# A recurrent transformer block with streamed weights: the residual in a home of its own, a larger GpSimd descriptor scratch, a quarter of an output unit kept in SBUF, and other places for the streamed units

## The chip, the cores and the metric

The kernel runs on one core of a Trainium2 chip. Its time is the device time of one execution in microseconds. Three executions before the change took 1982.02 us (median; 1969.82 to 1986.7).

## What is computed

`x` has 2048 rows of 1024 numbers, in bfloat16. It is layer-normalised to `xn`. Two branches are added to it. Branch B is a dense layer, a GELU and a second dense layer. Branch A goes through the rows in 64 segments of 32, one after the other: eight memory rows that the segment before left are put ahead of its rows, 32 heads of 128 attend over the 40 rows, and the first eight rows of the result are the memory of the next segment.

```python
x = A_x
xn = _layernorm(x, axis=-1)
return x + _A_ref(xn, A_mem0, A_Wq, A_Wk, A_Wv, A_Wo, A_seg_len) + _B_ref(xn, B_w1, B_b1, B_w2, B_b2)

# _A_ref, for each segment s
xs = x[:, s * seg_len:(s + 1) * seg_len, :].copy()
h = jnp.concatenate([mem, xs], axis=1)
q = jnp.einsum('btd,dhe->bhte', h, Wq)
k = jnp.einsum('btd,dhe->bhte', h, Wk)
v = jnp.einsum('btd,dhe->bhte', h, Wv)
scores = jnp.einsum('bhqe,bhke->bhqk', q, k) * scale
scores = jnp.where(mask[None, None], scores, -1000000000.0)
p = _softmax(scores, axis=-1)
o = jnp.einsum('bhqk,bhke->bhqe', p, v)
o = jnp.einsum('bhte,hed->btd', o, Wo)
mem = o[:, :M, :].copy()
outs.append(o[:, M:, :])
```

## The kernel before

The first stage (to about 464 us, with the first segment inside it) computes the layer norm and branch B, and leaves in DRAM what the segments need: the turned rows of each segment and the sum of `x` and branch B, as `hr_d` (128 x 512 a segment; the first 256 columns are turned rows, the last 256 the residual) and `hrL_d`, the same for the "left" rows.

The second stage is the loop over the 64 segments. A segment's product works on 32 rows: 24 of its own and the 8 memory rows. The last 8 rows of a segment are "left" over; those of four segments are gathered to another 32 rows and go through the same weights once in four segments. So segments come in four kinds, s mod 4: kind 0 multiplies left rows with the second half of K and the first of V, kind 1 with the first half of Q and the whole output matrix, kind 2 with the second half of Q, kind 3 with the first half of K and the second of V. Some left products are led, that is done ahead, at the end of the segment before (`lead_products`).

The four weight matrices are cut into 64 units of 128 x 2048 (512 KB), passed in the order K0, Q0, K1, Q1, V0, V1 (eight units each) and then 16 units of O (`pass_order`, L57). They do not all fit in SBUF. 46 units are resident; 18 are streamed, at the places marked S in `PLACED` (L72). Six slots (`STREAM_BUFS`) hold streamed units. When TensorE has used a streamed unit, `unit_done` (L669) calls `start_stream` (L235), which fills the slot that came free with the streamed unit six further on. Two of the 18 (`IN_PSUM`, the fourth, and `IN_BANKS`, the last) are kept turned in PSUM banks and are copied back by two VectorE copies each (L242); they start three units later (`LATER`). The other 16 come from DRAM by DMAs on SP's queue (L246). For one of them, `HALF`, the first 1024 columns stay in SBUF (`half_home`), and only the other 1024 are streamed (L244).

Around the change the order is set by three things. The slots of the stream, as told. The four 128-partition homes at the low end of SBUF: `half_home`, `pr_all`, `pd_main` and `hr_home`. And GpSimd's queue, which issues its DMAs strictly in the order of the program: a DMA that waits holds up all behind it. `SCRATCH` is the room, in bytes per partition, for the descriptors that GpSimd writes for its DMAs.

`pr_all` has two users in turn. `scores` (L803) writes the exponentials of the two halves of the heads to it (L823), VectorE masks them (L828), `sums` (L831) multiplies them into `pd_main` and `pd_left` (L857, L861), with TensorE's sums at L836 and L842. Then `load_res` (L961) loads the segment's residual into the same bytes (L964), VectorE adds the output product psX to it (L1012), and GpSimd stores it from there: for kinds 0 and 3 by four DMAs to the output (L1051), for kind 2 to `outM_d` (L1044) and from there by two DMAs of 4 x 12 rows (L1048), for kind 1, together with the left rows' residual, to `outL_d` (L1017) and from there to the output (L1042). The left residual is loaded into `pd_main` after the eighth output unit (L992). DMAs from DRAM to DRAM are put in the queue `small` and issued one or two at a time after a streamed unit (L675); in segments 1 to 4 it also holds copies of the sums for the last rows (L446).

The rows of the next segment are loaded into `hr_home` when the last V product is done (L254, on GpSimd from segment 5 on). After the output products ScalarE copies psX (L997), TensorE turns the memory rows (`put_mem`, L277), VectorE copies them into `hr_home` (L281), and the next segment's products (L709) can start.

The identity for TensorE's transposes lies in `pr_all` during the first stage.

Of the kernel before, what the change touches and what calls it, by code (L numbers as in the profile page):

```python
# [10 lines left out]
BF16 = mybir.dt.bfloat16  # L11
# [6 lines left out]
P = 128  # L18
S = 2048
DM = 1024  # L20
# [17 lines left out]
NX = 24  # L38
NL = SEG - NX
# [6 lines left out]
NUNIT = 64  # L46
STREAMED = 18
LOW = 3
SCRATCH = 352
SMALL = 3744  # L50
LEAD = 6
LATER = 3
STREAM_BUFS = 6
AT_BANKS, AT_HALF = 5, 2


def pass_order():  # L57
# [11 lines left out]


ORDER = pass_order()
PLACED = "S....S.." "..S....S" "...S...S" "...S...S" "....S..." ".S.S..S." ".S..S..S" "..S..S.S"  # L72
IS_STREAMED = {unit: PLACED[n] == "S" for n, unit in enumerate(ORDER)}
assert PLACED.count("S") == STREAMED
RESIDENT = [unit for unit in ORDER if not IS_STREAMED[unit]]
# [1 line left out]
IN_PSUM = [unit for unit in ORDER if IS_STREAMED[unit]][3]  # L77
STREAMED_O = [unit for unit in ORDER[48:] if IS_STREAMED[unit]]

IN_BANKS, HALF = STREAMED_O[AT_BANKS], STREAMED_O[AT_HALF]  # L80
KEPT = (IN_PSUM, IN_BANKS)
assert len(RESIDENT) == NUNIT - STREAMED

# [2 lines left out]
def kernel(  # L86
# [16 lines left out]
    nc = tc.nc  # L103
# [10 lines left out]
    Wo_v = A_Wo.rearrange("h e d -> e h d")  # L114
# [20 lines left out]
    }  # L135

    half_home = nc.alloc_sbuf_tensor_at("half_home", [P, DM], BF16, offset=SCRATCH)
    pr_all = nc.alloc_sbuf_tensor_at("pr_all", [P, 256], BF16, offset=SCRATCH + 2048)
    pd_main = nc.alloc_sbuf_tensor_at("pd_main", [P, 320], BF16, offset=SCRATCH + 2560)
    hr_home = nc.alloc_sbuf_tensor_at("hr_home", [P, 256], BF16, offset=SCRATCH + 3200)  # L140
    small_consts = nc.alloc_sbuf_tensor_at("small_consts", [P, 16], BF16, offset=SCRATCH + 3712)

    bd, off = small_consts[:, 0:4], small_consts[:, 4:8].bitcast(F32)

# [10 lines left out]

    qL_last = consts.tile([P, 16, SEG], BF16, name="qL_last")
    qL = [consts.tile([P, 16, SEG], BF16, name="qL"), qL_last]
    ident = pr_all[:, 0:P]
    make_identity(nc, ident)
    ident_mem = consts.tile([P, 4, NL], BF16, name="ident_mem")  # L160
    nc.vector.tensor_copy(out=ident_mem[:, :, :], in_=ident.rearrange("p (j t) -> p j t", j=4)[:, :, NX:SEG])
# [2 lines left out]
    for j in range(4):  # L164
        q = slice(32 * j, 32 * j + 32)
# [32 lines left out]
    for k in range(7):  # L198
# [4 lines left out]


    copies = {
        unit: dram.tile([P, 1024 if unit == HALF else 2048], BF16, name="Wc_" + "_".join(map(str, unit)))[:, :]
        for unit in reversed(ORDER) if IS_STREAMED[unit] and unit not in KEPT
    }

    def fetch(t, unit):  # L210
        w, i, u = unit
        if unit == HALF:
            nc.sync.dma_start(out=t, in_=Wo_v[:, 4 * i + 2 * u + 1, :])
        elif w == "O":
            h = 4 * i + 2 * u
            nc.sync.dma_start(out=t.rearrange("p (h d) -> p h d", d=DM), in_=Wo_v[:, h:h + 2, :])
        else:
            nc.sync.dma_start(out=t, in_=W_v[w][:, i, 2048 * u:2048 * u + 2048])
# [16 lines left out]
    def start_stream(slot):  # L235
        if not starts:
            return
        n = starts.popleft()
        unit, t = streams[n], slab(slot)
        if unit in kept_in:  # L240
            for c0, bank in kept_in[unit]:
                nc.vector.tensor_copy(out=t[:, c0:c0 + 1024], in_=bank)  # L242
        elif unit == HALF:
            nc.sync.dma_start(out=t[:, 1024:2048], in_=copies[unit])  # L244
        elif unit in copies:
            nc.sync.dma_start(out=t[:, :], in_=copies[unit])  # L246
        else:
            fetch(t[:, :], unit)
        stream_tiles[n], slot_of[n] = t, slot
# [357 lines left out]
    with tc.tile_pool(name="late", bufs=1) as late, \  # L607
# [3 lines left out]
        small = deque()  # L611
# [73 lines left out]
        for s in range(NSEG):  # L685
# [145 lines left out]
            def sums(u):  # L831
                prA, prB = st["pr", u]
                dA = mixed[:, 0:160].rearrange("p (c q) -> p c q", q=40)
                for j in range(4):
                    q = slice(32 * j, 32 * j + 32)
                    nc.tensor.matmul(  # L836
                        dA[q, :, :], lhsT=bd[:, j:j + 1].to_broadcast([P, 32]), rhs=prA, start=True, stop=False,
                        skip_group_check=True, tile_position=(0, 32 * j),
                    )
                for j in range(4):  # L840
                    q = slice(32 * j, 32 * j + 32)
                    nc.tensor.matmul(  # L842
                        ends(dA[q, :, :]), lhsT=bd[:, j:j + 1].to_broadcast([P, 32]),
                        rhs=prB.rearrange("p c (a b) -> p c a b", b=NL),
                        start=False, stop=True, skip_group_check=True, tile_position=(0, 32 * j),
                    )
                nc.scalar.activation(out=mixed[:, 0:160], in_=mixed[:, 0:160], func=ACT.Ln)

                for b in (1, 0):
                    nc.scalar.activation(  # L850
                        out=mixed[:, 160 * b:160 * b + 160], in_=mixed[:, 0:160], func=ACT.Exp, scale=-1.0,
                        bias=off[:, b:b + 1],
                    )
                pdA = pd_main.rearrange("p (c b q) -> p c b q", c=4, b=2)
                pdB = sp.tile([P, 128], BF16, name="pd_left").rearrange("p (c b a q) -> p c b a q", c=4, b=2, q=NL)
                dd = mixed[:, 0:320].rearrange("p (b c q) -> p b c q", b=2, q=40)
                nc.vector.tensor_tensor(  # L857
                    out=pdA.rearrange("p c b q -> p b c q"), in0=prA[:, None, :, :].to_broadcast([P, 2, 4, 40]),
                    in1=dd, op=ALU.mult,
                )  # L860
                nc.vector.tensor_tensor(  # L861
                    out=pdB.rearrange("p c b a q -> p b c a q"),
                    in0=prB.rearrange("p c (a q) -> p c a q", q=NL)[:, None, :, :, :].to_broadcast([P, 2, 4, 2, NL]),
                    in1=dd.rearrange("p b c (e q) -> p b c e q", q=NL)[:, :, :, ::4, :], op=ALU.mult,
                )
                st["pd", u] = pdA, pdB
# [26 lines left out]
            def o_product(unit, t, acc):  # L893


                (w, i, u), n = unit, 512 if left_o else 256
                lhs = outs[i // 4] if left_o else outs[i // 4][:, :, m0:m0 + SEG]
                for k in range(2):
                    w_k = half_home if unit == HALF and k == 0 else t[:, 1024 * k:1024 * k + 1024]
                    for jq in range(DM // n):  # L900
                        r = n // 8 * jq
                        nc.tensor.matmul(  # L902
                            acc[r:r + n // 8, 0:n],
                            lhsT=lhs[:, 4 * (i % 4) + 2 * u + k, :],
                            rhs=w_k[:, n * jq:n * jq + n],
                            start=(unit == O_UNITS[0] and k == 0),
                            stop=(unit == O_UNITS[-1] and k == 1),
                            tile_position=(0, r),
                        )
# [7 lines left out]
            if first:  # L917
                keep(IN_BANKS, 1024, d_oL, 2)
                keep(IN_BANKS, 0, half_home, 3)
                nc.sync.dma_start(out=half_home[:, :], in_=Wo_v[:, 4 * HALF[1] + 2 * HALF[2], :])  # L920
                copy_bits(mixed[:, 468:512].bitcast(U32), mask.bitcast(U32))
                for t in outs:
                    nc.vector.memset(t[:, :, 0:32], 0.0)
                turn_qL(psQL, 0)
# [34 lines left out]
                at[1] = [lambda: values(0, (0, 1))]  # L959

            def load_res():  # L961
                st["res"] = pr_all
                eng = nc.scalar if s < 5 else nc.gpsimd
                eng.dma_start(out=st["res"][:, :], in_=hr_d[s + 1, :, 256:512])  # L964

# [18 lines left out]
            for n, unit in enumerate(O_UNITS):  # L984
                t = unit_tile(unit)
                o_product(unit, t, psX)
                unit_done(unit)
                for fn in at.get(n, ()):
                    fn()
                if n == 7 and left_o:  # L990
                    st["resL"] = pd_main[:, 0:256]
                    nc.gpsimd.dma_start(out=st["resL"][:, :], in_=hrL_d[og, :, 256:512])  # L992
            nw = 2 if left_o else 1
            if not final:
# [13 lines left out]
                    lead_products(LEAD)  # L1008
            res, rows = st["res"], slice(s * SEG, s * SEG + NX)
            tiles = (res, st["resL"]) if left_o else (res,)  # L1010
            for w, r in enumerate(tiles):
                nc.vector.tensor_tensor(out=r[:, :], in0=psX[:, 256 * w:256 * w + 256], in1=r[:, :], op=ALU.add)  # L1012
                if left_o and not final:

                    for b in range(2):
                        c0 = 256 * (2 * b + w)
                        nc.gpsimd.dma_start(out=outL_d[og, :, c0:c0 + 256], in_=r[64 * b:64 * b + 64, :])  # L1017
# [25 lines left out]
            elif i4 == 2:  # L1043
                nc.gpsimd.dma_start(out=outM_d[g, :, :], in_=res[:, :])  # L1044
                o = out_flat[rows, :].rearrange("t (j c) -> j t c", j=4)
                r = outM_d[g, :, :].rearrange("(j t) c -> j t c", j=4)[:, 0:NX, :]
                for t in (slice(0, NX // 2), slice(NX // 2, NX)):
                    small.append(lambda o=o[:, t, :], r=r[:, t, :]: nc.gpsimd.dma_start(out=o, in_=r))  # L1048
            else:
                for j in range(4):  # L1050
                    nc.gpsimd.dma_start(out=out_flat[rows, 256 * j:256 * j + 256], in_=res[32 * j:32 * j + NX, :])  # L1051
# [37 lines left out]
```

The softmax here doesn't subtract the row's maximum and nothing guards it: scores larger than these inputs give would overflow.

## Time and profile before

| | |
|---|---|
| executions before | 1982.02 us median, 1969.82 to 1986.7 |
| profiled execution | 1987.94 us; span of its instructions 1986.2 us |
| mean granted TensorE clock | 0.983 |
| DMA in all | 220283 packets, 610.03 MB, mean 307 GB/s |
| HBM | 591.00 MB read, 30.21 MB written |
| segments 1 to 63 | 464.4 to 1980.7 us |
| streamed pieces | 512 KB x 960, 256 KB x 64 |
| L254 on GpSimd, issue to landing | 5.7 us median, 58 times |
| L964 on GpSimd, issue to landing | 5.7 us median, 59 times |
| L1051, one DMA of four | 514 ns on GpSimd, 4.6 us to landing |
| L1048, one DMA of two | 649 ns on GpSimd, 5.7 us to landing |
| L242, one copy of two | 683 ns on VectorE |

How to read it: PE is TensorE's matmuls, PEld its weight loads, DVE VectorE, ACT ScalarE, POOL GpSimd, SP SyncE. A line of the waits names the engine, the tile and line that waited, after the arrow what ended the wait, then the sum in us, the times and the longest. "issue" stands where the profile shows nothing that was waited for. A row of the busy time by stretch has the stretch, its length, the busy time of PE, PEld, DVE, ACT and POOL with the instructions in brackets, the granted clock as a share of full speed, the DMA engines' busy share and GB/s. A row of the timeline has start and length in us, engine, line, operation, tiles, count, and in square brackets the idle time of the engine before it and what ended it.

### The profile page before, as it was taken

To read this page: it belongs to the slowest core of one execution; us is meant where nothing else is said; L and a number is where in the kernel's file an instruction comes from. 1 tells how busy PE (TensorE), PEld (TensorE's weight loads), DVE (VectorE), ACT (ScalarE), POOL (GpSimd) and SP (SyncE) were. 2 spreads that over 40 slices of the span, in tenths; PEclk is the share of its full clock that TensorE was granted. 3 is DMA by queue.
4 is the path that set the end of the run, shared out by engine and by line. 5 is a ranking of instruction groups with operands and counts; after the bars stand their busy time and mean duration, and the time that the engine had idled before them with its cause. 6 is when DMAs were issued, how large, how long until landed. Compare 5 with 4: busy or idle time off the path is not lost. (4 is left out here: it accounts for less than half of the span.)

```text
span 1986.2 us, 73232 instructions
## 1 busy us (share of the span) xinstructions
PE 1747.1 (88%) x32275; PEld 938.2 (47%) x32275; DVE 918.9 (46%) x2222; ACT 638.5 (32%) x1356; POOL 286.6 (14%) x554
## 2 busy tenths in 40 slices
PE   7999999987878888998988888888888989888887
PEld 3444444444444454555544545454444445444443
DVE  6656565323434444444444444444444444444443
ACT  6343434212222332333333233233232333223232
POOL 0000000002331111111111121111111111111111
PEclk9999999989899999999999999999999999999999
DMA  9821212888889999999999999999999999899997
GB/s 329 243 55 42 56 41 56 305 321 308 290 317 342 349 360 339 373 368 373 347 376 356 349 374 341 353 362 363 347 356 341 386 357 375 326 358 356 339 359 294
DMA packets 220283, 610.03 MB, mean 307 GB/s; under 512 B 47675, under 2 KB 65771, under 8 KB 219948
## 3 DMA queue, kind: packets, MB, share of 16 engines
q1 hardware_dynamic: 199036, 585.18, 80.0%
q0 software_dynamic: 16832, 17.52, 2.8%
q8 instruction: 253, 4.15, 0.8%
q10 hardware_dynamic: 4096, 2.64, 0.4%
q14 instruction: 66, 0.54, 0.1%
HBM read 591.00 MB, written 30.21 MB: 313 GB/s over the span
## 5 line engine op out<-in xcount | busy, mean ns | idle before, releaser
L709 PE MATMUL acc<-u,hr_home 128*32 128x512 bf16 x11520 | 791.8, 387 | 60.7 <-DVE hr_home L281 21.3
L709 PEld LDWEIGHTS <-hr_home 128*32 128x32 bf16 x12288 | 345.6, 98 | 360.3 <-issue 62.4
L709 PE MATMUL acc<-u,hrL 128*32 128x512 bf16 x2880 | 256.4, 389 | 22.4 <-issue 8.2
L498 PE MATMUL ps<-u 128*128 128x512 bf16 x896 | 195.6, 381 | 2.6 <-ACT u L382 2.6
L902 PE MATMUL acc<-u,d_oL 128*32 128x256 bf16 (+1 forms) x3330 | 173.2, 290 | 18.8 <-DMA u<-Wc_O 15.9
L242 DVE COPY u<-kept 128x1024 bf16<-128x1024 bf16 x254 | 163.0, 683 | 16.0 <-PE acc L902 7.2
L902 PEld LDWEIGHTS <-b_oL 128*32 128x32 bf16 (+1 forms) x3552 | 108.9, 99 | 86.4 <-issue 50.0
L902 PE MATMUL acc<-u,b_oL 128*32 128x256 bf16 (+1 forms) x1776 | 119.0, 291 | 31.9 <-DMA u<-Wc_O 24.3
L547 PE MATMUL ps<-u 128*128 128x512 bf16 x672 | 147.0, 379 | 0.0
L498 PEld LDWEIGHTS <-u 128*128 128x128 bf16 x896 | 88.0, 98 | 108.9 <-issue 3.4
L902 PEld LDWEIGHTS <-d_oL 128*32 128x32 bf16 (+1 forms) x3552 | 104.4, 98 | 68.5 <-issue 28.2
L857 DVE TENSOR_TENSOR pd_main<-pr_all,mixed 128x320 bf16<-128x320 bf16 x128 | 61.9, 484 | 143.6 <-ACT mixed L850 141.5
L709 PEld LDWEIGHTS <-hrL 128*32 128x32 bf16 x3072 | 85.4, 97 | 86.5 <-issue 24.5
L767 DVE STREAM_TRANSPOSE b_oL<-b_oL 128x512 bf16<-128x512 bf16 x128 | 90.5, 707 | 63.4 <-ACT b_oL L753 63.4
L828 DVE TENSOR_TENSOR pr_all<-pr_all,mixed 128x96 bf16<-128x96 bf16 (+1 forms) x256 | 37.9, 189 | 166.1 <-ACT pr_all L823 166.1
L753 ACT CAST kT<-acc 128x512 bf16<-128x512 f32 x64 | 37.5, 585 | 237.2 <-PE acc L709 237.2
L902 PE MATMUL acc<-W_O,b_oL 128*32 128x256 bf16 (+1 forms) x1776 | 106.2, 289 | 6.1 <-issue 6.1
L753 ACT CAST b_oL<-acc 128x512 bf16<-128x512 f32 x128 | 75.2, 587 | 109.9 <-PE acc L709 109.9
L254 POOL DMA_DIRECT2D hr_home<-hr_d x58 | 33.1, 571 | 488.8 <-PE acc L709 394.0
L547 PEld LDWEIGHTS <-u 128*128 128x128 bf16 x672 | 65.3, 98 | 77.4 <-DVE g_u L514 0.4
L281 DVE CAST hr_home<-mixed 128x64 bf16<-128x64 f32 x63 | 14.1, 225 | 186.6 <-PE mixed L277 120.1
L997 ACT CAST d_oL<-acc 128x256 bf16<-128x256 f32 (+1 forms) x63 | 26.8, 426 | 221.3 <-PE acc L902 221.3
(132 smaller groups left out, 2120.7 us busy)
## 6 DMA issues: line engine op xcount, KB each, us to landing
u<-Wc_K SPq DMA_DIRECT2D x256, 512.0 KB
u<-Wc_V SPq DMA_DIRECT2D x256, 512.0 KB
u<-Wc_O SPq DMA_DIRECT2D x256, 512.0 KB
u<-Wc_Q SPq DMA_DIRECT2D x192, 512.0 KB
u<-Wc_O SPq DMA_DIRECT2D x64, 256.0 KB
u<-in_B_w_dram SPq DMA_DIRECT2D x14, 512.0 KB
u<-in_A_Wq_dram SPq DMA_DIRECT2D x13, 512.0 KB
u<-in_A_Wv_dram SPq DMA_DIRECT2D x12, 512.0 KB
```

The lines of the kernel that those rows point to most:

```text
L242: nc.vector.tensor_copy(out=t[:, c0:c0 + 1024], in_=bank)
L254: eng.dma_start(out=hr_home[:, :], in_=hr_d[s, :, 0:256])
L281: nc.vector.tensor_copy(out=hT[:, :, NX:SEG].rearrange("p (j c) t -> p j c t", c=nc_), in_=psM.rearrange("p c j t -> p j c t"),)
L498: nc.tensor.matmul(ps[:, :].rearrange("p (s t) -> p s t", t=SEG), lhsT=w1_sb[fb // 14 * 8 + kt][:, (fb % 14) * P:(fb % 14 + 1) * P], rhs=x ...
L547: nc.tensor.matmul(ps[:, :], lhsT=gts[fc // 4][:, fc % 4, t * P:(t + 1) * P], rhs=w2_sb[fc // 2][:, fc % 2, cs], start=(fc == 0), stop=(fc ...
L709: nc.tensor.matmul(o, lhsT=lhs[:, i, :], rhs=m, start=(i == seq[0]), stop=(i == seq[-1]), tile_position=(0, 32 * j),)
L753: cp(out=out, in_=ps.rearrange("p (h e) -> p h e", e=32))
L767: nc.vector.transpose(out=home, in_=home)
L828: nc.vector.tensor_tensor(out=p, in0=p, in1=m[:, None, :].to_broadcast([P, 4, n]), op=ALU.min)
L857: nc.vector.tensor_tensor(out=pdA.rearrange("p c b q -> p b c q"), in0=prA[:, None, :, :].to_broadcast([P, 2, 4, 40]), in1=dd, op=ALU.mult,)
L902: nc.tensor.matmul(acc[r:r + n // 8, 0:n], lhsT=lhs[:, 4 * (i % 4) + 2 * u + k, :], rhs=w_k[:, n * jq:n * jq + n], start=(unit == O_UNITS[ ...
L997: nc.scalar.copy(out=o_sb[:, 0:no, :], in_=psX[:, 0:32 * no].rearrange("p (h e) -> p h e", e=32))
```

## The change

`SCRATCH` grows from 352 to 512 bytes and `SMALL` shrinks by as much. `half_home` is shared out: columns 0 to 511 hold a quarter of one streamed output unit (`PART`, the fifth streamed O unit, instead of half of the third), 512 to 767 the residual (`res_home`), 768 to 1023 `pr_all`. The left rows' residual is loaded into `pr_all` instead of `pd_main`, after the second output unit instead of the eighth, and the two residuals are added and stored in the reverse order. `pd_left` gets a fixed place, the identity lies in `pd_main`. Kind 2's store of 4 x 24 rows is one DMA instead of two. The 18 streamed units have other places: before 0, 5, 10, 15, 19, 23, 27, 31, 36, 41, 43, 46, 49, 52, 55, 58, 61, 63 (15 and 63 kept in PSUM, 55 half kept in SBUF), after 0, 1, 7, 12, 17, 21, 25, 31, 36, 41, 43, 46, 51, 53, 55, 58, 61, 62 (12 and 62 kept in PSUM, a quarter of 61 kept in SBUF). Each engine executes as many products and elementwise instructions as before; GpSimd issues 16 DMAs fewer.

```diff
@@ -46,12 +46,13 @@
 NUNIT = 64
 STREAMED = 18
 LOW = 3
-SCRATCH = 352
-SMALL = 3744
+SCRATCH = 512
+SMALL = 3584
 LEAD = 6
 LATER = 3
 STREAM_BUFS = 6
-AT_BANKS, AT_HALF = 5, 2
+AT_BANKS, AT_PART = 5, 4
+PART_COLS = 512
 
 
 def pass_order():
@@ -69,7 +70,7 @@
 
 
 ORDER = pass_order()
-PLACED = "S....S.." "..S....S" "...S...S" "...S...S" "....S..." ".S.S..S." ".S..S..S" "..S..S.S"
+PLACED = "SS.....S" "....S..." ".S...S.." ".S.....S" "....S..." ".S.S..S." "...S.S.S" "..S..SS."
 IS_STREAMED = {unit: PLACED[n] == "S" for n, unit in enumerate(ORDER)}
 assert PLACED.count("S") == STREAMED
 RESIDENT = [unit for unit in ORDER if not IS_STREAMED[unit]]
@@ -77,7 +78,7 @@
 IN_PSUM = [unit for unit in ORDER if IS_STREAMED[unit]][3]
 STREAMED_O = [unit for unit in ORDER[48:] if IS_STREAMED[unit]]
 
-IN_BANKS, HALF = STREAMED_O[AT_BANKS], STREAMED_O[AT_HALF]
+IN_BANKS, PART = STREAMED_O[AT_BANKS], STREAMED_O[AT_PART]
 KEPT = (IN_PSUM, IN_BANKS)
 assert len(RESIDENT) == NUNIT - STREAMED
 
@@ -135,10 +136,12 @@
     }
 
     half_home = nc.alloc_sbuf_tensor_at("half_home", [P, DM], BF16, offset=SCRATCH)
-    pr_all = nc.alloc_sbuf_tensor_at("pr_all", [P, 256], BF16, offset=SCRATCH + 2048)
+    hr_home = nc.alloc_sbuf_tensor_at("hr_home", [P, 256], BF16, offset=SCRATCH + 2048)
     pd_main = nc.alloc_sbuf_tensor_at("pd_main", [P, 320], BF16, offset=SCRATCH + 2560)
-    hr_home = nc.alloc_sbuf_tensor_at("hr_home", [P, 256], BF16, offset=SCRATCH + 3200)
-    small_consts = nc.alloc_sbuf_tensor_at("small_consts", [P, 16], BF16, offset=SCRATCH + 3712)
+    pd_left = nc.alloc_sbuf_tensor_at("pd_left", [P, 128], BF16, offset=SCRATCH + 3200)
+    small_consts = nc.alloc_sbuf_tensor_at("small_consts", [P, 16], BF16, offset=SCRATCH + 3456)
+
+    part_home, res_home, pr_all = half_home[:, 0:PART_COLS], half_home[:, 512:768], half_home[:, 768:1024]
 
     bd, off = small_consts[:, 0:4], small_consts[:, 4:8].bitcast(F32)
 
@@ -155,7 +158,7 @@
 
     qL_last = consts.tile([P, 16, SEG], BF16, name="qL_last")
     qL = [consts.tile([P, 16, SEG], BF16, name="qL"), qL_last]
-    ident = pr_all[:, 0:P]
+    ident = pd_main[:, 0:P]
     make_identity(nc, ident)
     ident_mem = consts.tile([P, 4, NL], BF16, name="ident_mem")
     nc.vector.tensor_copy(out=ident_mem[:, :, :], in_=ident.rearrange("p (j t) -> p j t", j=4)[:, :, NX:SEG])
@@ -203,14 +206,16 @@
 
 
     copies = {
-        unit: dram.tile([P, 1024 if unit == HALF else 2048], BF16, name="Wc_" + "_".join(map(str, unit)))[:, :]
+        unit: dram.tile([P, 2048 - PART_COLS if unit == PART else 2048], BF16, name="Wc_" + "_".join(map(str, unit)))[:, :]
         for unit in reversed(ORDER) if IS_STREAMED[unit] and unit not in KEPT
     }
 
     def fetch(t, unit):
         w, i, u = unit
-        if unit == HALF:
-            nc.sync.dma_start(out=t, in_=Wo_v[:, 4 * i + 2 * u + 1, :])
+        if unit == PART:
+            h = 4 * i + 2 * u
+            nc.sync.dma_start(out=t[:, 0:DM - PART_COLS], in_=Wo_v[:, h, PART_COLS:])
+            nc.sync.dma_start(out=t[:, DM - PART_COLS:], in_=Wo_v[:, h + 1, :])
         elif w == "O":
             h = 4 * i + 2 * u
             nc.sync.dma_start(out=t.rearrange("p (h d) -> p h d", d=DM), in_=Wo_v[:, h:h + 2, :])
@@ -240,8 +245,8 @@
         if unit in kept_in:
             for c0, bank in kept_in[unit]:
                 nc.vector.tensor_copy(out=t[:, c0:c0 + 1024], in_=bank)
-        elif unit == HALF:
-            nc.sync.dma_start(out=t[:, 1024:2048], in_=copies[unit])
+        elif unit == PART:
+            nc.sync.dma_start(out=t[:, PART_COLS:], in_=copies[unit])
         elif unit in copies:
             nc.sync.dma_start(out=t[:, :], in_=copies[unit])
         else:
@@ -852,7 +857,7 @@
                         bias=off[:, b:b + 1],
                     )
                 pdA = pd_main.rearrange("p (c b q) -> p c b q", c=4, b=2)
-                pdB = sp.tile([P, 128], BF16, name="pd_left").rearrange("p (c b a q) -> p c b a q", c=4, b=2, q=NL)
+                pdB = pd_left.rearrange("p (c b a q) -> p c b a q", c=4, b=2, q=NL)
                 dd = mixed[:, 0:320].rearrange("p (b c q) -> p b c q", b=2, q=40)
                 nc.vector.tensor_tensor(
                     out=pdA.rearrange("p c b q -> p b c q"), in0=prA[:, None, :, :].to_broadcast([P, 2, 4, 40]),
@@ -896,13 +901,13 @@
                 (w, i, u), n = unit, 512 if left_o else 256
                 lhs = outs[i // 4] if left_o else outs[i // 4][:, :, m0:m0 + SEG]
                 for k in range(2):
-                    w_k = half_home if unit == HALF and k == 0 else t[:, 1024 * k:1024 * k + 1024]
                     for jq in range(DM // n):
-                        r = n // 8 * jq
+                        r, c0 = n // 8 * jq, DM * k + n * jq
+                        w_t = part_home if unit == PART and c0 < PART_COLS else t
                         nc.tensor.matmul(
                             acc[r:r + n // 8, 0:n],
                             lhsT=lhs[:, 4 * (i % 4) + 2 * u + k, :],
-                            rhs=w_k[:, n * jq:n * jq + n],
+                            rhs=w_t[:, c0:c0 + n],
                             start=(unit == O_UNITS[0] and k == 0),
                             stop=(unit == O_UNITS[-1] and k == 1),
                             tile_position=(0, r),
@@ -917,7 +922,7 @@
             if first:
                 keep(IN_BANKS, 1024, d_oL, 2)
                 keep(IN_BANKS, 0, half_home, 3)
-                nc.sync.dma_start(out=half_home[:, :], in_=Wo_v[:, 4 * HALF[1] + 2 * HALF[2], :])
+                nc.sync.dma_start(out=part_home, in_=Wo_v[:, 4 * PART[1] + 2 * PART[2], 0:PART_COLS])
                 copy_bits(mixed[:, 468:512].bitcast(U32), mask.bitcast(U32))
                 for t in outs:
                     nc.vector.memset(t[:, :, 0:32], 0.0)
@@ -959,7 +964,7 @@
                 at[1] = [lambda: values(0, (0, 1))]
 
             def load_res():
-                st["res"] = pr_all
+                st["res"] = res_home
                 eng = nc.scalar if s < 5 else nc.gpsimd
                 eng.dma_start(out=st["res"][:, :], in_=hr_d[s + 1, :, 256:512])
 
@@ -987,8 +992,8 @@
                 unit_done(unit)
                 for fn in at.get(n, ()):
                     fn()
-                if n == 7 and left_o:
-                    st["resL"] = pd_main[:, 0:256]
+                if n == 1 and left_o:
+                    st["resL"] = pr_all
                     nc.gpsimd.dma_start(out=st["resL"][:, :], in_=hrL_d[og, :, 256:512])
             nw = 2 if left_o else 1
             if not final:
@@ -1008,7 +1013,7 @@
                     lead_products(LEAD)
             res, rows = st["res"], slice(s * SEG, s * SEG + NX)
             tiles = (res, st["resL"]) if left_o else (res,)
-            for w, r in enumerate(tiles):
+            for w, r in reversed(list(enumerate(tiles))):
                 nc.vector.tensor_tensor(out=r[:, :], in0=psX[:, 256 * w:256 * w + 256], in1=r[:, :], op=ALU.add)
                 if left_o and not final:
 
@@ -1044,8 +1049,7 @@
                 nc.gpsimd.dma_start(out=outM_d[g, :, :], in_=res[:, :])
                 o = out_flat[rows, :].rearrange("t (j c) -> j t c", j=4)
                 r = outM_d[g, :, :].rearrange("(j t) c -> j t c", j=4)[:, 0:NX, :]
-                for t in (slice(0, NX // 2), slice(NX // 2, NX)):
-                    small.append(lambda o=o[:, t, :], r=r[:, t, :]: nc.gpsimd.dma_start(out=o, in_=r))
+                small.append(lambda o=o, r=r: nc.gpsimd.dma_start(out=o, in_=r))
             else:
                 for j in range(4):
                     nc.gpsimd.dma_start(out=out_flat[rows, 256 * j:256 * j + 256], in_=res[32 * j:32 * j + NX, :])
```

## The prediction, made before the changed kernel was run

> **What bounds the kernel now.** I read the page first, then the busy time by stretch, then who waited for whom on TensorE, then GpSimd's timeline.
>
> ```profile
> span 1986.2 us, 73232 instructions
> PE 1747.1 (88%) x32275; PEld 938.2 (47%) x32275; DVE 918.9 (46%) x2222; ACT 638.5 (32%) x1356; POOL 286.6 (14%) x554
> q1 hardware_dynamic: 199036, 585.18, 80.0%
> ```
>
> TensorE is busiest, but the weight stream (q1) moves 585.18 MB in 80.0% of 1986.2 us: 368 GB/s while it moves. The stretches below follow segment ends (last output product, L902): segments 2, 3, 4, then 5 to 60 (14 groups of four).
>
> ```profile
> 489.80:518.70 28.90, 21.47 (x484) 11.31 (x481) 10.52 (x26) 7.36 (x17) 9.82 (x18) 0.88 0.83 289
> 518.70:547.40 28.70, 23.02 (x511) 12.48 (x504) 10.67 (x25) 7.36 (x17) 7.96 (x14) 0.88 0.84 305
> 547.40:578.20 30.80, 22.26 (x508) 12.67 (x504) 10.68 (x25) 7.35 (x17) 14.76 (x27) 0.89 0.78 279
> 578.20:1909.10 1330.90, 1159.07 (x26544) 653.11 (x26536) 595.73 (x1414) 412.42 (x952) 218.19 (x406) 0.99 0.96 357
> ```
>
> The last columns are granted clock, DMA share, GB/s. In the long stretch the DMA engines work 0.96 of the time, TensorE 0.87: DMA bounds it, TensorE is close behind. Adding packet durations per group of four: 95.07 us = 91.3 DMA work + 3.76 idle. By segment kind (s mod 4 = 0, 1, 2, 3) the idle time is 2.41, 0.35, 0.66, 0.23 us. Segments 2 to 4 are 5 to 7 us longer than the average of 23.8, with the DMA idle for 4.9 + 4.6 + 6.8 = 16.3 us.
>
> TensorE's waits in 578.2:1909.1, then in 489.8:578.2:
>
> ```profile
> PE acc L902 <- DMA u<-Wc_O: 35.3, 52, 2.6
> PE acc L709 <- DVE hr_home L281: 18.6, 13, 3.2
> PE mixed L836 <- DVE pr_all L828: 18.3, 19, 2.7
> PE acc L709 <- DVE pd_main L1012: 15.1, 12, 2.2
> PE acc L709 <- DVE pr_all L1012: 4.0, 5, 1.3
> ```
>
> ```profile
> PE mixed L836 <- DVE pr_all L828: 11.9, 2, 7.3
> PE acc L709 <- DVE pd_main L1012: 4.8, 1, 4.8
> ```
>
> The first is the bound itself. The other four come from GpSimd's queue and the shared home pr_all. ScalarE shows why L836 is late: the exponential may not overwrite pr_all before the store of the residual has read it.
>
> ```profile
> DMA out_dram<-pr_all: 38.2, 19
> ```
>
> GpSimd's timeline shows a segment of kind 3, then one of kind 1:
>
> ```profile
> 1100.81 0.55 POOL L1044 DMA_DIRECT2D outM_d<-pr_all  x1 [6.92 <-DVE pr_all L1012]
> 1106.03 0.65 POOL L1048 DMA_DIRECT2D out_dram<-outM_d  x1 [4.67 <-DMA outM_d<-pr_all]
> 1113.17 0.65 POOL L1048 DMA_DIRECT2D out_dram<-outM_d  x1 [6.49 <-issue]
> 1118.74 0.59 POOL L254 DMA_DIRECT2D hr_home<-hr_d  x1 [4.93 <-DVE b_oL L890]
> ...
> 1163.65 0.55 POOL L254 DMA_DIRECT2D hr_home<-hr_d  x1 [12.13 <-PE acc L709]
> 1164.89 0.56 POOL L964 DMA_DIRECT2D pr_all<-hr_d  x1 [0.69 <-DVE pd_left L861]
> 1169.35 0.54 POOL L992 DMA_DIRECT2D pd_main<-hrL_d  x1 [3.91 <-PE acc L902]
> ```
>
> In kind 3 the second half of the store starts 7.1 us after the first, and the next segment's rows (L254) 5.6 us after that. The output products had begun at 1115.25, so L254 came 3.5 us after them; over all kind 3 segments 2.9 us on average, against 0.5 to 0.7 in the others. In kind 1 the third load (L992) starts 5.7 us after the first, the median landing time of L254.
>
> **What the Trainium skill says.** "DMA: Bandwidth & Descriptors", Terms: a descriptor is 16 B. So SCRATCH 352 is 22 places, 512 is 32. The same page, The descriptor swizzle: a 128-partition transfer puts 8 data and 1 completion descriptors on each engine. Why a DMA increments its semaphore by 16 and not by 1: the count of engines divides the slowest dimension, so a 4x12x256 store uses 4 engines, 12 + 1 each. Two halves are 26, three loads 27: neither fits in 22. The trace agrees: both are issued one landing (5.2 to 5.7 us) apart. "TensorE: Matmul & The Clock Gate", Part 1: after idling the array runs at half clock in windows of 3.4 us. The trace agrees: after the 2.11 us wait at the end of this kind 3 segment the clock is 0.66 for 5 us, the DMA share 0.69.
>
> **The change part by part**, against the execution's own 1986.2 us span (1987.9 with what lies around it; the median of three is 1982.0).
>
> 1. A quarter instead of a half kept: the streamed piece grows from 256 to 384 KB, 131072 B more in each of 64 segments. At 368 GB/s 0.36 us, 1.4 per group. It lands in the bound: 14 x 1.4 = 20 us in the long stretch, about 2.5 elsewhere. Below: 0.30 us, by the packets' medians (84 ns for 2 KB, 159 for 4 KB, so about 121 for 3 KB; 8 per engine); above 0.36. DMA work becomes 92.7 per group. TensorE, product counts unchanged, could then do a group in 82.8 busy + 12.0 waits - 2.9 for the stream - 4.0 removed (below) = 87.9. So DMA stays the bound.
>
> 2. Own home for the residual: L964 no longer waits for L861 (about 1 us earlier), and L823 no longer for the out store. This removes L836's 18.3 us and L1012's 4.0 in the long stretch, 11.9 in segments 3 and 4. In kind 1 pr_all takes the left residual instead, whose store is now issued first (the reversed loop); it lands in about 4 us, and the exponential comes some 9 us later. Cost nothing; if that cover went, it would be the present L836 wait in one segment of four, up to 1.4 us.
>
> 3. 31 descriptors: one 4x24x256 store takes 24 + 1 places and fits. The store leaves one landing earlier, and L254 in kind 3 is issued when the last V product ends, 2.3 us sooner. Its landing ends L281, so the 18.6 us wait goes, and the half clock behind it. The three loads (27) fit too: L992, at n == 1, goes out about 3 us sooner, which covers most of the 15.1 us of pd_main L1012 (1.3 each) and the 4.8 in segment 2, where it also passes three to six queued L446 copies. Late next: L254's own landing, already as long as a short output pass (6 us against 5.2 to 6.5); lead products cover it.
>
> 4. Kept units' copies (L242, 1.37 us for two): used at places 12 and 62 instead of 15 and 63, started after place 0 and 55. Seven products x 0.22 = 1.5 us still cover the latter; L242 waits are 4.0 us now, and I bound the loss by 0.22 per segment, 14 in all. TensorE has 4.8 per group to spare: hidden. If that cover is gone, 14 us.
>
> 5. New places: same 18 units. Waits for Wc_O sit at 49, 52 and 61; the first two move to 51 and 53 and get looser. 0, 1, 7 release slots earlier than 0, 5, 10, just where kind 0 idles. But 58, 61, 62, 0, 1 are dense. The trace has no price for it. Bounds: -0.6 per group (the idle time 4 to 9 us into kind 0 gone even without part 3) to +1 (every boundary a wait of 0.25). I take 0.
>
> Sum. Removed TensorE waits: 56.0 us, 4.0 per group; they help only where the DMA idles. Kind 0's 2.41 us lie in two places, 1.0 at 4 to 9 us after the boundary (parts 2, 3: gone) and 1.1 at 15 to 22 us, in the doubled V pass, where places don't change (stays). Kinds 1 to 3 keep 0.2 each. Idle 1.7 per group: 92.7 + 1.7 = 94.4, -0.67, x 14 = -9.4. Segments 2 to 4: 88.4 becomes 3 x (24.0 + 0.36 + 0.5) = 74.6, -13.8. Segments 1 and 61 to 63: +1.4. Together -21.8: span 1964.4, -1.1%. Against the median of 1982.0: 1960.
>
> **Rivals.** Changes of 1% (20 us) are about what a measurement of this kernel can tell from none.
>
> A (forecast), stream-bound with 1.7 idle: 1960, own range 1950 to 1970. Chance 0.45.
> B, the stream never pauses (0.5 idle per group): 14 x 1.2 = 17 less, 1943. For: kinds 1 and 3 reach 0.23 to 0.35 already. Against: the doubled V pass. Chance 0.18.
> C, the idle time doesn't shrink in the long stretch, because removed waits become waits for Wc_O: +20 there, -13.8 + 1.4 elsewhere: +7, 1989. For: Wc_O waits are the largest already. Against: idle time follows the late L281. Chance 0.15.
> D, slower: six buffers don't cover the dense run 58, 61, 62, 0, 1; TensorE stops at every boundary, clock halves, and later the stream fills and pauses. It decides from 4.8 idle per group, 1.0 above today's: 14 x (92.7 + 4.8 - 95.07) = +34, -12.4 elsewhere: +22, 2004. Against: 8.4 us of prefetch (six x 1.4). Chance 0.12.
> E, descriptor room is not what holds L254, and it stays late: kind 0 keeps its 1.0 us: +14, 1974. For: the profile calls the wait only "issue". Against: three loads and two halves agree with 22 places. Chance 0.10.
>
> **How the numbers follow.** Faster by over 1% (below 1962): 0.26 of A, all of B, 0.02 of E: 0.46. Slower by over 1% (above 2002): D and 0.03 of C for unpriced placement: 0.15. The rest, 0.39. The range reaches from B's 1943 less 5 to C's 1989 plus 7, leaving D and some of B outside: 1938 to 1996.
>
> **What would show it.** Right: DMA share 0.98 in the long stretch, segments 2 to 4 near 25 us each, L836 and L281 gone from TensorE's waits, L254 within 0.7 us of the output products in kind 3, waits for Wc_O or Wc_K grown in their place. Wrong: L254 still late (E), DMA share at 0.96 with higher Wc waits (C, D), or more than 0.4 us of DMA work per segment for the quarter.

## The result, and the profile after

The changed kernel takes 1897.5 us (median of four executions, 1888.7 to 1902.73) against 1984.36 us for the kernel before (four executions, 1969.82 to 1989.31). The ratio is 0.957, with a 95% interval of 0.951 to 0.963: 4.3% faster. The forecast of 1960 us, and its range down to 1938, held too little. The direction was right, the size was not: 22 us were forecast and 87 us measured.

The profiled execution is the fastest of the four, 1888.7 us with a span of 1887.0. That of before, 1987.94 us, is near the slowest of its kernel. So the two traces lie 99 us apart where the medians lie 87 apart; differences that are taken from the traces add up to 12 us more than that of the medians. The page of the changed kernel:

```profile
span 1887.0 us, 72995 instructions
PE 1729.5 (92%) x32255; PEld 940.0 (50%) x32275; DVE 921.3 (49%) x2222; ACT 637.6 (34%) x1356; POOL 277.2 (15%) x538
q1 hardware_dynamic: 199292, 593.57, 83.0%
```

The stream moves 8.4 MB more, 593.57 MB instead of 585.18, as the quarter in place of the half demands.

The busy time by stretch, cut at the segment ends of the changed kernel: segments 2, 3 and 4, then 5 to 60. Lines are shifted by four or five from here on (L907 is L902 of before, L714 is L709, L286 is L281, L1052 is L1048).

```profile
489.10:510.70 21.60, 18.73 (x487) 10.99 (x483) 10.59 (x26) 7.56 (x18) 9.87 (x18) 1.00 1.03 399
510.70:533.30 22.60, 20.67 (x512) 12.31 (x508) 10.79 (x25) 7.31 (x18) 7.91 (x14) 1.00 1.02 389
533.30:555.50 22.20, 20.43 (x510) 14.04 (x506) 10.89 (x25) 7.22 (x17) 13.72 (x25) 1.00 1.03 400
555.50:1813.60 1258.10, 1149.65 (x26544) 653.70 (x26536) 597.66 (x1414) 411.58 (x952) 209.79 (x392) 1.00 1.00 383
```

Three columns answer to the rows of before. The granted clock is 1.00 throughout, where it was 0.88 to 0.89 in the three early segments. The DMA share is 1.00 and above (packets that overlap are added), where it was 0.78 to 0.84 and 0.96. And the rate, which counts all DMAs of the core, is 383 to 400 GB/s, where it was 279 to 305 and 357. Segments 2 to 4 take 66.4 us instead of 88.4, segments 5 to 60 take 1258.1 instead of 1330.9.

| Stretch | before, us | after, us | difference |
|---|---|---|---|
| to the end of segment 0 | 464.4 | 465.6 | +1.2 |
| segment 1 | 25.4 | 23.5 | -1.9 |
| segments 2 to 4 | 88.4 | 66.4 | -22.0 |
| segments 5 to 60 | 1330.9 | 1258.1 | -72.8 |
| segments 61 to 63 | 71.6 | 67.6 | -4.0 |
| rest | 5.5 | 5.8 | +0.3 |

TensorE's largest waits in segments 5 to 60, and three small ones that are used below:

```profile
PE acc L714 <- issue: 17.5, 27, 1.9
PE mixed L816 <- DVE b_oL L772: 15.8, 25, 0.7
PE acc L907 <- DMA u<-Wc_O: 13.2, 36, 0.9
PE acc L714 <- DMA u<-Wc_K: 11.9, 23, 1.2
PE acc L907 <- issue: 9.7, 14, 1.7
PE mixed L816 <- DVE mixed L645: 8.4, 13, 0.7
PE acc L907 <- DVE u L247: 8.1, 13, 0.7
PE acc L714 <- DVE kL L758: 1.3, 6, 0.2
PE acc L714 <- DMA u<-Wc_Q: 1.2, 4, 0.4
PE acc L714 <- DMA u<-Wc_V: 1.2, 2, 0.7
```

The lines of before that answer to these, beside those of the prediction:

```profile
PE acc L709 <- issue: 14.8, 19, 1.9
PE acc L902 <- issue: 11.0, 12, 2.3
PE acc L709 <- DVE kL L753: 7.7, 14, 0.7
PE acc L902 <- DVE u L242: 4.0, 8, 0.5
PE acc L709 <- DMA u<-Wc_Q: 2.6, 6, 0.9
PE acc L709 <- DMA u<-Wc_V: 2.0, 4, 1.0
PE acc L709 <- DMA u<-Wc_K: 1.2, 2, 0.9
```

The four waits that the prediction removed are gone, but for 0.3 us: 18.6 us for L281, 18.3 for L836, 15.1 and 4.0 for the two L1012 (lines of before). Over the whole second stage two short remnants are left:

```profile
PE acc L714 <- DVE hr_home L286: 2.0, 4, 1.0
PE mixed L841 <- DVE half_home L833: 0.8, 1, 0.8
```

The waits for the stream did not grow in their place. Together (O, K, Q and V) they were 41.1 us in segments 5 to 60 and are 27.5. The exponential no longer waits for the stores of kinds 0, 2 and 3. This is what ScalarE's L828 (L823 of before) still waits for among stores. It is that of kind 1, where `pr_all` holds the left residual; the profile has one name, `half_home`, for both residuals:

```profile
DMA outL_d<-half_home: 8.9, 10
```

GpSimd's timeline of the changed kernel, a segment of kind 3 and then one of kind 1, answers to the one of before:

```profile
1054.09 0.55 POOL L1049 DMA_DIRECT2D outM_d<-half_home  x1 [7.23 <-DVE half_home L1017]
1060.37 0.71 POOL L1052 DMA_DIRECT2D out_dram<-outM_d  x1 [5.74 <-DMA outM_d<-half_home]
1069.54 0.57 POOL L259 DMA_DIRECT2D hr_home<-hr_d  x1 [8.46 <-PE acc L714]
1070.11 0.53 POOL L969 DMA_DIRECT2D half_home<-hr_d  x1
...
1114.63 0.55 POOL L259 DMA_DIRECT2D hr_home<-hr_d  x1 [12.17 <-PE acc L714]
1115.33 0.55 POOL L969 DMA_DIRECT2D half_home<-hr_d  x1
1116.20 0.55 POOL L997 DMA_DIRECT2D half_home<-hrL_d  x1 [0.33 <-issue]
```

One store (L1052) stands where two halves stood 7.1 us apart. The load of the next segment's rows (L259) now waits for TensorE's last V product and for nothing else. Over the kind 3 segments it comes 0.4 us after the first output product instead of 2.9. The three loads of kind 1 go out within 1.6 us; before, the third came 5.7 us after the first. In kind 1 the third load is issued 2.0 us after the output products begin, where it was 6.4.

### The profile page after: what moved, and what is told of

Same layout as the page of the kernel before. It is cut to its first block, busy times and chain, and to the rows that moved or that the text cites. A ratio compares the mean times of both kernels' runs of the same rounds, so it can differ in the third digit from the quotient of the medians.

```text
span 1887.0 us, 72995 instructions
## 1 busy us (share of the span) xinstructions
PE 1729.5 (92%) x32255; PEld 940.0 (50%) x32275; DVE 921.3 (49%) x2222; ACT 637.6 (34%) x1356; POOL 277.2 (15%) x538
## 3 DMA queue, kind: packets, MB, share of 16 engines
q1 hardware_dynamic: 199292, 593.57, 83.0%
## 4 chain that ended last, share of the span: by engine, by line
PE 67%; DMA 19%; DVE 7%; ACT 3%; issue 3%; POOL 0%; ACTq 0%; DVEq 0%; POOLq 0%; SPq 0%
PE acc L714 32%; PE ps L503 10%; PE acc L907 10%; DMA u<-Wc_K 9%; PE ps L552 8%; DMA u<-Wc_O 5%; DMA u<-Wc_Q 3%; PE ps L587 2%; ACT mixed L855 2%; PE acc L881 2%; DVE b_oL L772 1%; DMA outL_d<-half_home 1%; DVE pd_main L862 1%; PE mixed L816 1%; DVE u L247 1%
## 5 line engine op out<-in xcount | busy, mean ns | idle before, releaser
L714 PE MATMUL acc<-u,hr_home 128*32 128x512 bf16 x11520 | 781.5, 382 | 32.4 <-DMA u<-Wc_K 13.6
L714 PEld LDWEIGHTS <-hr_home 128*32 128x32 bf16 x12288 | 350.8, 97 | 321.5 <-issue 72.1
L714 PE MATMUL acc<-u,hrL 128*32 128x512 bf16 x2880 | 256.3, 381 | 12.4 <-issue 6.1
L907 PE MATMUL acc<-u,d_oL 128*32 128x256 bf16 (+1 forms) x3552 | 177.2, 292 | 12.3 <-DMA u<-Wc_O 7.9
L907 PEld LDWEIGHTS <-b_oL 128*32 128x32 bf16 (+1 forms) x3552 | 109.1, 98 | 75.0 <-issue 40.9
L907 PEld LDWEIGHTS <-d_oL 128*32 128x32 bf16 (+1 forms) x3552 | 104.4, 99 | 63.8 <-issue 20.7
L862 DVE TENSOR_TENSOR pd_main<-half_home,mixed 128x320 bf16<-128x320 bf16 x128 | 62.5, 488 | 150.1 <-ACT mixed L855 147.6
L907 PE MATMUL acc<-u,b_oL 128*32 128x256 bf16 (+1 forms) x1665 | 108.7, 290 | 19.3 <-DVE u L247 8.8
L714 PEld LDWEIGHTS <-hrL 128*32 128x32 bf16 x3072 | 90.4, 96 | 66.3 <-issue 24.7
L907 PE MATMUL acc<-W_O,b_oL 128*32 128x256 bf16 (+1 forms) x1776 | 108.3, 289 | 4.9 <-issue 4.6
L259 POOL DMA_DIRECT2D hr_home<-hr_d x58 | 32.7, 564 | 528.7 <-PE acc L714 528.7
L833 DVE TENSOR_TENSOR half_home<-half_home,mixed 128x96 bf16<-128x96 bf16 (+1 forms) x256 | 37.6, 188 | 127.4 <-ACT half_home L828 127.3
L855 ACT ACTIVATE mixed<-mixed,small_consts 128x160 f32<-128x160 f32 x256 | 94.3, 368 | 8.4
```

Source lines behind the costliest of these rows:

```text
L714: nc.tensor.matmul(o, lhsT=lhs[:, i, :], rhs=m, start=(i == seq[0]), stop=(i == seq[-1]), tile_position=(0, 32 * j),)
L833: nc.vector.tensor_tensor(out=p, in0=p, in1=m[:, None, :].to_broadcast([P, 4, n]), op=ALU.min)
L855: nc.scalar.activation(out=mixed[:, 160 * b:160 * b + 160], in_=mixed[:, 0:160], func=ACT.Exp, scale=-1.0, bias=off[:, b:b + 1],)
L862: nc.vector.tensor_tensor(out=pdA.rearrange("p c b q -> p b c q"), in0=prA[:, None, :, :].to_broadcast([P, 2, 4, 40]), in1=dd, op=ALU.mult,)
L907: nc.tensor.matmul(acc[r:r + n // 8, 0:n], lhsT=lhs[:, 4 * (i % 4) + 2 * u + k, :], rhs=w_t[:, c0:c0 + n], start=(unit == O_UNITS[0] and k ...
```

## Experiments

None of the experiments was run. So nothing here rests on a run that undoes one part of the change, and the causes are read from the two traces alone. Four kernels would each bear on one question. They are described here, with the expectations that were written for them, because the questions stay open. (A fifth, the kernel before with the new places alone, would have asked the first question from the other side. It was not run either.) Three dots in an edit mark lines left out.

The changed kernel with the places of before:

```diff
-PLACED = "SS.....S" "....S..." ".S...S.." ".S.....S" "....S..." ".S.S..S." "...S.S.S" "..S..SS."
+PLACED = "S....S.." "..S....S" "...S...S" "...S...S" "....S..." ".S.S..S." ".S..S..S" "..S..S.S"
```

> The changed kernel with the streamed units at the places of before (0, 5, 10, 15, 19, ... 63; a quarter of 61 kept in SBUF). Theory W (the gain is TensorE's removed waits, with the clock behind them; the weight stream was not the bound): places hardly matter, within 1% of the changed kernel, 1880 to 1915 us, ratio to before 0.95 to 0.965. Theory P (the new places feed the stream better): at least half of the 87 us comes back, 1940 us or more, and the waits for Wc_O at 49 and 52 return.

Not measured. The share of the places stays open.

The changed kernel with the residual in `pr_all` again:

```diff
-                st["res"] = res_home
+                st["res"] = pr_all
...
-                if n == 1 and left_o:
-                    st["resL"] = pr_all
+                if n == 7 and left_o:
+                    st["resL"] = pd_main[:, 0:256]
...
-            for w, r in reversed(list(enumerate(tiles))):
+            for w, r in list(enumerate(tiles)):
```

> The changed kernel with the residual in pr_all again (left rows' residual in pd_main after the eighth output unit, stored in the order of before); 31 descriptors, one store for kind 2 and the new places stay. Theory W (the gain is TensorE's removed waits, with the clock behind them; the weight stream was not the bound): the wait of L836 for the store returns (18.3 us in segments 5 to 60 and 11.9 in segments 3 and 4 before), and part of the 24 us of psX waits: 25 to 55 us slower than the changed kernel, 1922 to 1952 us. Theory P (the new places feed the stream better, and that is the gain): within 1% of the changed kernel, under 1917 us.

Not measured. It would have priced the home of its own, together with the place and the order of the left residual.

The changed kernel with 24 places for descriptors and two stores:

```diff
-SCRATCH = 512
-SMALL = 3584
+SCRATCH = 384
+SMALL = 3712
...
-                small.append(lambda o=o, r=r: nc.gpsimd.dma_start(out=o, in_=r))
+                for t in (slice(0, NX // 2), slice(NX // 2, NX)):
+                    small.append(lambda o=o[:, t, :], r=r[:, t, :]: nc.gpsimd.dma_start(out=o, in_=r))
```

> The changed kernel with 384 bytes (24 places) of descriptor scratch, and two stores of 4 x 12 rows for kind 2; own home and new places stay. Theory W: L254 of kind 3 is late again by about 2 us, L281 waits 18 us, half clock behind it, the third load waits for a landing again: 25 to 50 us slower than the changed kernel, 1922 to 1947 us. Theory R (descriptor room is not what holds the queue): within 1%, and L254 of kind 3 within 0.7 us of the output products.

Not measured. It would have priced the descriptor room together with the merged store.

The kernel before with less to stream:

```diff
...
         elif unit == HALF:
-            nc.sync.dma_start(out=t[:, 1024:2048], in_=copies[unit])
+            pass
...
-                    w_k = half_home if unit == HALF and k == 0 else t[:, 1024 * k:1024 * k + 1024]
+                    w_k = half_home if unit == HALF else t[:, 1024 * k:1024 * k + 1024]
```

> The kernel before with 256 KB less to stream in each segment: the half of unit 55 that was streamed isn't, and its products read the half that is kept, so that one head's output weights stand for two (that part of the result is left out); 384 bytes of scratch, small constants at another place. Theory S (the prediction's floor: the weight stream bounds the kernel before at 368 GB/s): 0.7 us less DMA work in each of 64 segments, 30 to 45 us faster than before, 1940 to 1955 us. Theory W (TensorE's waits for GpSimd's queue and for pr_all set the pace, and the stream waits for TensorE): waits for Wc_O shrink, but 20 us faster at most, 1962 us or more.

Not measured. That the stream could go faster than the prediction's floor rests on the trace of the changed kernel, told below.

## Why the prediction was wrong

**Part 2, own home: right.** L836 and L1012 no longer wait. The cover that the prediction named for the left residual in `pr_all` held: the exponential waits 8.9 us in all, ten times, and TensorE's L841 once, 0.8 us.

**Part 3, descriptors: the effect right, the cause argued.** GpSimd's queue was held by landings, and the trace of before shows this more closely than the prediction said. The second half of the store was issued 0.30 to 0.31 us after the first had landed, 16 times out of 16. The next segment's rows (L254) followed the landing of the second half by 0.30 to 0.31 us, 14 times out of 14 in segments 5 to 60. The third load (L992) followed the landing of the first by 0.32 to 0.33 us, again 14 times out of 14, also where the profile names a product of TensorE as what ended the wait. In the changed kernel the third load goes out 3.0 to 4.3 us before the first has landed. The number of DMAs in flight was not the limit, for the four stores of L1051 went out within 2.1 us and took 4.6 us to land. Nor were their bytes, for two loads of 64 KB went out together (L254 and L964 of kind 3) where two stores of 24 KB did not. That leaves the room for descriptors as the likely limit. The prediction's count agrees with these waits, but it has two holes. The second half and the load behind it are 13 + 9 = 22 places, as many as 352 bytes hold by the same count, and the load waited all the same. And 26 for two halves takes both to lie on the same four engines, while the section that the prediction cites for the four lets a transfer from GpSimd on fewer than 16 take the next engines in turn; the traces don't name a packet's engine. Besides, the changed kernel has one store for two, and its third load stands earlier in the program. No run changes the room alone, so its part in the gain is not shown. E, in which L254 stays late, did not come true.

**The half clock: the place right, the size left out.** The prediction saw it and gave it no number. The Trainium skill, "TensorE: Matmul & The Clock Gate", Part 1, says that the array falls to half clock after idling, in windows of 3.4 us. The clock's own records show ten such windows in segments 5 to 60 before and two after; in segments 2 to 4 three double ones before and none after. The page speaks of an idle window; here TensorE had been busy for 0.5 to 1.9 us of the 3.4 us before each of the ten. A window costs up to half its length, so the eight that are gone cost up to 14 us, and the early ones up to 10. How it looks on the page, a few us after a kind 3 segment's end, first before, then after:

```profile
1124.67:1129.67 5.00, 5.00 (x68) 2.19 (x64) 2.41 (x5) 0.58 (x1) 2.04 (x4) 0.66 0.69 230
```

```profile
1078.67:1083.67 5.00, 4.89 (x124) 2.79 (x117) 2.19 (x6) 1.57 (x4) 0.30 (x1) 1.00 1.03 394
```

Both rows have TensorE busy nearly all the time. The 68 products of the first are all 128 x 512 wide. Of the 124 of the second, 92 are; the others are the small products of the scores. So 68 wide products stand against 92, at a clock of 0.66 against 1.00. A slowed engine looks busy; only the clock column and the count of like products tell. The DMA rate is lower with it, 230 GB/s against 394. That fits slots that come free at TensorE's pace, but these rows don't prove it.

**Parts 4 and 5, copies and places: small, both as bounded.** Waits for the kept units' copies rose from 4.0 to 8.1 us in segments 5 to 60, at most 0.7 us each: less than the 14 us bound. At the dense run the waits for Wc_K rose from 1.2 to 11.9 us, most of them at place 1. That is D's mechanism, but only 0.2 us a boundary on average, and without the half clock and the pauses of the stream that D added to it. The waits for Wc_O fell from 35.3 to 13.2. Of the 35.3, 20 stood at place 61, which is streamed in both kernels, and 3 stand there now, with a piece of 384 KB for one of 512. How much of the fall is due to the places and to the smaller piece at 61, and how much to the steadier stream, the two traces can't tell.

**The step that failed** is the sum per group of four segments, 92.7 us of DMA work and 1.7 idle, and with it "So DMA stays the bound" and the rule that the removed waits "help only where the DMA idles". A group took 1258.1 / 14 = 89.9 us, with 0.5 MB more streamed: less than the DMA work alone was to take. By the prediction's own measure, the sum of packet durations, it is 90.0 us of work and an idle time of -0.1 (below zero, because packets that overlap are added). So both terms were too large: the work by 2.7 us a group, 38 us in 14 groups, and the idle time by 1.8, 25 us. Together that is the whole miss in this stretch, 72.8 - 9.4 = 63.4 us. Rival B had the pauses gone but kept the floor.

The idle term failed in kind 0. Its idle time fell from 2.4 to 0.2 us; also the 1.1 us in the doubled V pass, which were to stay because the places there don't change, fell, to 0.4.

The work term failed in what it took a packet's duration for. The quarter's own price was right: its packets of 3 KB took 129 ns on average where those of 2 KB took 87, which is 0.34 us a segment against the 0.36 forecast. But the 91.3 us were carried over as a fixed amount of work. A 4 KB packet of the stream had the same median before and after, 159 ns. Its mean fell from 173.9 to 168.5 ns, because fewer packets were slow, and that is 2.6 us a group. In the trace of before, a 4 KB packet took 183 ns on average when 14 or 15 packets had been in flight 0.2 us earlier, and 168 ns with 16. With fewer than four it was 381 ns, but only 174 of 107520 packets were such. What the packets took beyond 159 ns while fewer than 16 were in flight adds up to 3.9 us per group before and 1.9 after. So most of the extra duration that went lay where the stream was thin. That such a packet's duration holds a part of the pause is a reading of these numbers; the trace does not say what a slow packet waited for.

The same can be read without the single packets, from the rows by stretch: GB/s divided by the DMA share. Before, it is 289 / 0.83 = 348, 305 / 0.84 = 363 and 279 / 0.78 = 358 in segments 2 to 4, and 357 / 0.96 = 372 after that. In the changed kernel it is 383 / 1.00 and 399 / 1.03 = 387. A rate per busy time that rises with the busy share says that the share is not a share of a fixed capacity. The mix of packets doesn't explain it: with each packet at the median of its size the quotient would be 396 to 405 in all these stretches. The prediction had the rows of before on the page, divided one sum by another instead (585.18 MB by 80.0% of the span), and took 368 for a ceiling. The Trainium skill, "DMA: Bandwidth & Descriptors", Bandwidth, has 341 GB/s for 1 MB and 425 for 16 MB of single transfers; all the core's DMAs together moved 383 over 1258 us here, and 400 in a segment.

**TensorE's ledger** says where the time went from the other side, for its busy and idle time fill the stretch. Per group it was 82.8 us busy and 12.3 idle; it is 82.1 busy (1149.65 / 14) and 7.8 idle. Over segments 5 to 60 the busy time fell by 9.4 us, which fits the half clock that is gone, and the idle time by 63.4. By what ended the waits: the four that were to be removed fell by 55.7 us, those for the stream by 13.6 and the wait of L709 for kL by 6.4, while those for the copies rose by 4.1 and those named "issue" by 8.5. The prediction's sum let 9.4 + 20 (the extra bytes) = 29 of 56.0 us count. In segments 2 to 4 the busy time fell by 6.9 us and the idle time by 15.1, against 13.8 forecast in all. Segments 1 and 61 to 63, forecast at 1.4 us more, take 5.9 less.

By kind, a group became shorter by 3.0, 0.5, 1.5 and 0.2 us (kinds 0 to 3). Kind 0 begins with the wait for L281 (17.8 of its 18.6 us lie there), and kind 2 with that for L1012 on pd_main (all 15.1). So the gain lies where the removed waits were. But the waits for Wc_O fell in these two kinds as well, by 12.7 and 8.2 us in 14 groups, so this does not part the waits from the places.

The two traces thus show TensorE's waits in the way before, and a stream whose pauses the busy share of 0.96 did not show in full. Whether the stream is the bound now is open. Its share is 1.00 and TensorE waits 27.5 us for it, but by the argument above the share proves nothing, and whether more bytes would now cost time in full was not tried.

**What stays open.** Of the gain in segments 5 to 60 the removed waits can be put to parts by what ended them: 22.3 us (L836 and L1012 on pr_all) to the home of its own, 33.7 (L281 and L1012 on pd_main) to the descriptor room, the merged store and the earlier load. That is a reading of who waited for whom, not a measurement of a part alone. The share of the new places is not known, and it is the rival that stands untested: the stream's waits fell as well. What the quarter's 131072 B cost in time, beyond the 0.34 us of DMA work in each segment, is not known either.

## What to carry to other kernels

A DMA busy share of 0.96 does not prove a bandwidth bound: divide the rate by the share in several stretches. If the quotient rises with the share, as it did here, the share is not a share of a fixed capacity, and the room can be larger than the idle time shows. Then don't discount a removed wait on the compute engine by the DMA's idle time; here almost all of it went from TensorE's idle time, and some half clock with it. When a software queue is late, compare the start of each DMA with the landings of those before it: a start that follows a landing by the same 0.3 us every time shows what it waited for, even where the profile names no releaser or another one.

## What the runs showed of the hardware that was not expected

The stream's rate is not fixed by packet size alone: with nearly the same packets and the same median of 159 ns for 4 KB, the core's DMAs moved 357 GB/s over 1331 us before and 383 GB/s over 1258 us after, and 389 to 400 GB/s in segments 2 to 4. The mean duration of a 4 KB packet differed with how many packets had been in flight 0.2 us earlier, 183 ns for 14 or 15 and 168 for 16. The half clock came without a fully idle window: TensorE had been busy for 0.5 to 1.9 of the 3.4 us before each of ten.
